# Dividing the first rows of an output projection unevenly over the DMA engines of a decode step

## The chip, the cores and the metric

The kernel runs on one core of a Trainium2 chip. The metric is the device time of one execution in microseconds (us). Before the change it is 197.57 us, the median of three runs that lie between 197.56 and 197.66. A profiled execution counts time from the first instruction to the last, and this span is 195.2 us.

Five engines of the core appear in the profile: PE (TensorE; its weight loads are listed apart as PEld), DVE (VectorE), ACT (ScalarE), POOL (GpSimd) and SP (SyncE). SP computes nothing here. It starts nearly all transfers between HBM and on-chip memory, one after the other, on one queue. The transfers themselves run on 16 DMA engines.

## What is computed

One decode step for four sequences: a layer norm, then attention over a window of the last 4096 cached positions (32 query heads, 8 key/value heads, head size 128) beside a SwiGLU feed-forward block, with both results added to the input.

```python
W = min(4096, max(256, Sk // 4))          # 4096
xn = layernorm(A_x)                       # [4, 1, 512]
q = (xn @ wq)                             # 32 heads of 128
k = k_cache[:, :, Sk - W:, :]             # 8 heads, each used by 4 query heads
v = v_cache[:, :, Sk - W:, :]
p = softmax(einsum("bhqd,bhkd->bhqk", q, k) * 128 ** -0.5)
o = einsum("bhqk,bhkd->bhqd", p, v)
attention = o.reshape(4, 1, 4096) @ wo    # wo is [4096, 512]
ffn = (silu(xn @ w_gate) * (xn @ w_up)) @ w_down
out = A_x + attention + ffn
```

Everything is in bf16 in HBM. The used windows of K and V are 32 MB each in the page's count (16 transfers of 2048 KB each), W_Q and W_O are 4 MB each, and the three feed-forward weights 1.75 MB each: 81.01 MB are read from HBM in one execution.

## The kernel before

The 32 pairs of sequence and key/value head are worked through in 16 duos. For each duo one transfer brings K and one brings V. PE transposes K tile by tile, DVE copies the transposes to on-chip memory, PE makes the scores, ACT takes the exponential, and PE multiplies with V. Each of K and V has two buffers, so the transfer for a duo can start when the duo before the last has left its buffer.

SP's list of transfers, cut to its last part:

```python
def load_v(j):
    if j > 0:
        eng.wait_ge(s_pv, j)               # the product with the V before last is done
    a = j % NSL * KVN
    eng.dma_start(VB[:, a:a + KVN], kv_ap(A_v_cache, j)).then_inc(d_v[j % NSL], 16)

def load_wo(n):                            # chunk n of W_O
    a, b = WO_CUTS[n], WO_CUTS[n + 1]      # WO_CUTS = (0, 16, 24, 28, 31, 32), in units of [128, 512]
    if b - a > REP:                        # REP = 4
        o, i = WO[:, a // REP:b // REP].rearrange("p k e n -> p k (e n)"), wo_ap[:, a // REP:b // REP]
    else:
        ...                                # a chunk within one key/value head
    eng.dma_start(o, i).then_inc(d_wo[n], 16)

# ... W_Q, the first K, W_gate and W_up are started before this ...
for j in range(1, NDUO):                   # NDUO = 16
    load_k(j)
    load_v(j - 1)
    if j == 1:
        eng.dma_start(WD[:], wd_ap).then_inc(d_wd, 16)
load_wo(0)                                 # units 0 to 15: half of W_O
load_v(NDUO - 1)                           # the last V
for n in range(1, len(d_wo)):
    load_wo(n)                             # units 16-23, 24-27, 28-30, 31
eng.wait_ge(s_y, 1)
eng.dma_start(out_ap[0], y[0:B, :]).then_inc(d_out, 16)
```

W_O lies in on-chip memory as `WO[128, 8, 4, 512]`: partition, key/value head, unit e within the head, output column. For one key/value head a partition's row is 2048 elements (4 KB) and lies in one piece in HBM.

PE's list from the end of the loop over duos on:

```python
eng.wait_ge(s_gu4, 1)
# ... four transposes for the feed-forward block, permute(0, ...) of heads 0 to 6 ...
# ... x and the 28 products with W_down go to ps_acc ...
eng.wait_ge(s_pc, 1)
for q in range(4):
    wo(q)                                  # heads 0 to 3; wo(0) waits for chunk 0 of W_O
pv(NDUO // 2, 0)                           # the last V: waits for its transfer, 1 + 64 products
wo(4)                                      # waits for chunk 1 (units 16-23)
wo(5)
eng.wait_ge(s_nrm, NDUO + 2)               # DVE has normalized the last product
permute(1, HKV - 1, HKV)
wo(6)                                      # waits for chunk 2 (units 24-27)
eng.wait_ge(s_pc, 2)                       # DVE has copied the last permutation
last = wo(7)                               # waits for chunks 3 (units 28-30) and 4 (unit 31)
last.then_inc(s_acc, 1)                    # DVE then makes y, and SP and ACT store it
```

`wo(q)` is four times two products of [128, 4] with [128, 256], and waits where a chunk begins. `norm` on DVE, which follows `pv`, is a reduction, a reciprocal and a product.

Of the kernel before, what the change touches and what calls it, by code (L numbers as in the profile page):

```python
# [10 lines left out]
def bass_parallel_sum__sliding_block_cached__swiglu_ffn__decode_kernel(  # L11
# [10 lines left out]
    out: bass.AP,  # L22
):
    B, _, D = A_x.shape
    _, HKV, Sk, Dh = A_k_cache.shape
    HQ = A_wq.shape[1] // Dh
    F = B_w_gate.shape[1]
# [23 lines left out]
    WO = sb("wo_sb", [128, HKV, REP, D], BF16)  # L51
# [53 lines left out]
    def sem(name):  # L105
        return nc.alloc_semaphore(name=name)
# [3 lines left out]
    d_wu = sem("d_wu")  # L110
    d_wd = sem("d_wd")
    d_out = sem("d_out")
    WO_CUTS = (0, 16, 24, 28, 31, 32)
    d_wo = [sem("d_wo%d" % q) for q in range(len(WO_CUTS) - 1)]
    s_xc = sem("s_xc")
    s_ss = sem("s_ss")
    d_k = [sem("d_k%d" % s) for s in range(NSL)]
# [33 lines left out]
    wo_ap = A_wo.rearrange("(k p e) n -> p k (e n)", k=HKV, e=REP)  # L151
# [3 lines left out]
    def kv_ap(cache, j):  # L155
        b, kv = 2 * j % B, 2 * j // B
        return cache[b:b + 2, kv, Sk - W:, :].rearrange("i (p t) d -> p i (t d)", t=NT)

    with nc.Block() as block:

        @block.gpsimd
        def _(eng):
            eng.memset(ident[:], 0.0)
            eng.memset(I4[:], 0.0)
            eng.memset(I4w[:], 0.0)
            eng.memset(XnT[:], 0.0)
            eng.memset(ones[:], 1.0)
            eng.drain()
            eng.affine_select(I4[:], I4[:], pattern=[[-1, B]], compare_op=ALU.not_equal,
                              fill=1.0, base=0, channel_multiplier=1)  # L170
            eng.affine_select(ident[:], ident[:], pattern=[[-1, 128]], compare_op=ALU.not_equal,
                              fill=1.0, base=0, channel_multiplier=1)
            eng.drain()
            eng.tensor_copy(I4w[:, 0:B], I4[:])
            for h in range(REP):
                eng.tensor_copy(sel[:, :, h, :], ident[:].rearrange("p (m e) -> p e m", e=REP))
            eng.memset(even[:], 0.0)
            eng.drain()
            eng.affine_select(even[:], even[:], pattern=[[-2, 64]], compare_op=ALU.not_equal,
                              fill=1.0, base=0, channel_multiplier=1)  # L180
            for w in (32, 16, 8, 4, 2, 1):
                eng.drain()
                eng.tensor_tensor(even[:, 0:w], even[:, 0:w], even[:, w:2 * w], ALU.add)
            eng.drain()
            eng.tensor_scalar(off[:, 0:1], even[:, 0:1], 30000.0, -30000.0, ALU.mult, ALU.add)
            eng.tensor_scalar(off[:, 1:2], even[:, 0:1], -30000.0, None, ALU.mult)
            eng.memset(P[:], 1.0)
            eng.memset(VB[:, (NSL - 1) * KVN:], 0.0).then_inc(s_const, 1)  # L188

        @block.sync  # L190
        def _(eng):
            def load_k(j):
                if j >= NSL:
                    eng.wait_ge(s_tr, NG * (j - NSL + 1))
                a = j % NSL * KVN
                eng.dma_start(KB[:, a:a + KVN], kv_ap(A_k_cache, j)).then_inc(d_k[j % NSL], 16)  # L196

            def load_v(j):
                if j > 0:
                    eng.wait_ge(s_pv, j)  # L200
                a = j % NSL * KVN
                eng.dma_start(VB[:, a:a + KVN], kv_ap(A_v_cache, j)).then_inc(d_v[j % NSL], 16)  # L202

            def load_wo(n):
                a, b = WO_CUTS[n], WO_CUTS[n + 1]
                if b - a > REP:
                    o, i = WO[:, a // REP:b // REP].rearrange("p k e n -> p k (e n)"), wo_ap[:, a // REP:b // REP]
                else:
                    e, k = a % REP, a // REP
                    o = WO[:, k, e:e + b - a].rearrange("p e n -> p (e n)")  # L210
                    i = wo_ap[:, k, D * e:D * (e + b - a)]
                eng.dma_start(o, i).then_inc(d_wo[n], 16)  # L212

            eng.dma_start(WQ[:, 0:2], wq_ap[:, 0:2]).then_inc(d_wq[0], 16)
            eng.dma_start(WQ[:, 2:4], wq_ap[:, 2:4]).then_inc(d_wq[1], 16)  # L215
            load_k(0)
            eng.dma_start(WG[:], wg_ap).then_inc(d_wg, 16)  # L217
            eng.dma_start(WU[:], wu_ap).then_inc(d_wu, 16)
            for j in range(1, NDUO):
                load_k(j)  # L220
                load_v(j - 1)
                if j == 1:
                    eng.dma_start(WD[:], wd_ap).then_inc(d_wd, 16)
            load_wo(0)
            load_v(NDUO - 1)
            for n in range(1, len(d_wo)):
                load_wo(n)
            eng.wait_ge(s_y, 1)
            eng.dma_start(out_ap[0], y[0:B, :]).then_inc(d_out, 16)
            eng.wait_ge(d_out, 32)  # L230
# [90 lines left out]
        def _(eng):  # L321
# [67 lines left out]
            def wo(q):  # L389
                for e in range(REP):  # L390
                    if REP * q + e in WO_CUTS:
                        eng.wait_ge(d_wo[WO_CUTS.index(REP * q + e)], 16)
                    for n in range(2):
                        last = mm(ps_acc[64 * n:64 * n + B, 0:256], OP[:, e, q, :],  # L394
                                  WO[:, q, e, 256 * n:256 * n + 256], start=False,
                                  stop=(q == HKV - 1 and e == REP - 1), skip_group_check=True)
                return last
# [17 lines left out]
            for t in range(NF):  # L415
                g, i = TG[t]
                for n in range(2):
                    mm(ps_acc[64 * n:64 * n + B, 0:256], guT[:, i, g, :], WD[:, t, 256 * n:256 * n + 256],
                       start=False, stop=False, skip_group_check=True)
            eng.wait_ge(s_pc, 1)  # L420
            for q in range(4):
                wo(q)
            pv(NDUO // 2, 0)
# [36 lines left out]
```

## Time and profile before

| what | value |
|---|---|
| time, median of three | 197.57 us |
| span of the profiled execution | 195.2 us |
| read from HBM | 81.01 MB, 415 GB/s over the span |
| share of 16 DMA engines' time on SP's queue | 97.5% |
| busy: PE, PEld, DVE, ACT | 80%, 73%, 60%, 10% |
| mean granted PE clock | 0.843 |

The profile's page gives the busy time of each engine, the same in 40 slices of time, the DMA queues, the chain of work that ended last, and the costliest groups of instructions with what ended the idle time before them. A queue's "packets" are the single pieces that a DMA engine moves; the trace keeps start, duration and size of each, and for each transfer's semaphore the time of each of the 16 steps by which it counts up.

### The profile page before, as it was taken

What the parts mean: (1) busy time and instruction counts of PE and PEld (TensorE: products, weight loads), DVE (VectorE), ACT (ScalarE), POOL (GpSimd) and SP (SyncE); (2) the same over time, 40 slices, a digit from 0 to 9 for tenths busy, and PEclk for the clock granted to TensorE, in tenths of its full rate; (3) what the DMA queues carried; (4) which work ended last, traced back from release to release, by engine and by line L of the source; (5) the groups of instructions that cost most, each with busy time, mean ns of one, the idle gap of its engine ahead of it and who ended that gap; (6) DMA issues with size and microseconds to landing.
All of it is one profiled execution on the core that took longest, in us unless ns stands there. A gap on an engine that the chain in (4) does not pass through costs nothing.

```text
span 195.2 us, 7471 instructions
## 1 busy us (share of the span) xinstructions
PE 155.5 (80%) x3335; PEld 142.6 (73%) x3335; DVE 117.2 (60%) x199; ACT 20.0 (10%) x42; POOL 11.6 (6%) x28
## 2 busy tenths in 40 slices
PE   0007569987999797987799779797989777999884
PEld 0012139977999797986799679797989777999662
DVE  3780099673848485756386638484857573858213
ACT  5201300101010101010101010101010101010100
POOL 6880000000000000000000000000000000000000
PEclk9999757996679788899579969797888995769699
DMA  6999999999999999999999999999999999999991
GB/s 216 430 430 450 423 420 426 434 436 433 430 433 433 433 433 430 433 430 433 433 430 430 430 430 430 430 430 430 433 430 433 430 430 430 430 430 411 448 397 60
DMA packets 6589, 81.10 MB, mean 415 GB/s; under 512 B 684, under 2 KB 824, under 8 KB 1848
## 3 DMA queue, kind: packets, MB, share of 16 engines
q1 hardware_dynamic: 6568, 81.01, 97.5%
q8 instruction: 5, 0.08, 0.1%
q10 hardware_dynamic: 16, 0.01, 0.0%
HBM read 81.01 MB, written 0.00 MB: 415 GB/s over the span
## 4 chain that ended last, share of the span: by engine, by line
DMA 65%; PE 31%; SPq 2%; issue 1%; DVE 0%
DMA kbuf<-in_A_k_cache_dram 43%; PE ps_kt L360 25%; DMA wu_sb<-in_B_w_up_dram 12%; DMA wo_sb<-in_A_wo_dram 10%; PE ps_o L379 2%; PE ps_s L367 2%; PE ps_den L348 1%; SPq L212 1%; PE ps_den L376 0%; PE ps_acc L394 0%; SPq L196 0%; SPq L217 0%; SPq L202 0%; DVE y_sb L318 0%; SPq L215 0%
## 5 line engine op out<-in xcount | busy, mean ns | idle before, releaser
L279 DVE COPY kT<-ps_kt 128x1024 bf16<-128x1024 bf16 x128 | 81.9, 686 | 34.9 <-PE ps_kt L360 34.6
L360 PE MATMUL ps_kt<-ident,kbuf 128*128 128x128 bf16 x1024 | 81.9, 259 | 12.0 <-DMA kbuf<-in_A_k_cache_dram 11.9
L360 PEld LDWEIGHTS ps_kt<-ident,kbuf 128*128 128x128 bf16 x1024 | 79.0, 120 | 14.2 <-issue 6.9
L379 PEld LDWEIGHTS ps_o<-p,vbuf 128*128 128x128 bf16 x1088 | 29.8, 96 | 3.1 <-issue 1.0
L379 PE MATMUL ps_o<-p,vbuf 128*128 128x8 bf16 x1088 | 29.9, 166 | 1.0 <-issue 1.0
L250 ACT ACTIVATE p<-ps_s,off 128x256 bf16<-128x256 f32 x32 | 13.4, 471 | 144.3 <-PE ps_s L367 144.3
L367 PE MATMUL ps_s<-qT,kT 128*128 x1024 | 28.0, 166 | 0.0
L367 PEld LDWEIGHTS ps_s<-qT,kT 128*128 128x128 bf16 x1024 | 26.9, 96 | 0.0
L285 DVE TENSOR_REDUCE den<-ps_den 128x8 f32<-128x512 f32 x17 | 11.8, 692 | 20.4 <-PE ps_o L379 20.4
L326 PE MATMUL ps_o<-i,tmp 4*128 4x4 f32 x4 | 0.6, 254 | 14.2 <-DVE tmp L269 14.2
L326 PEld LDWEIGHTS ps_o<-i,tmp 4*128 4x128 f32 x4 | 0.6, 206 | 14.2 <-POOL vbuf L188 14.2
L376 PE MATMUL ps_den<-p,ones 128*128 128x512 bf16 x17 | 6.5, 382 | 3.4 <-DMA vbuf<-in_A_v_cache_dram 3.4
L269 DVE TENSOR_SCALAR tmp<-tmp,st_rstd 4x512 f32<-4x512 f32 x1 | 7.9, 7864 | 0.1
L188 POOL MEMSET vbuf<- 128x8192 bf16 x1 | 6.9, 6921 | 0.0
L394 PE MATMUL ps_acc<-wo_sb,oP 128*4 128x256 bf16 x64 | 4.2, 272 | 1.0 <-DMA wo_sb<-in_A_wo_dram 0.9
L376 PEld LDWEIGHTS ps_den<-p,ones 128*128 128x128 bf16 x17 | 1.7, 97 | 4.3 <-issue 4.0
L289 DVE TENSOR_TENSOR oT<-ps_o,den 128x8 f32 (+1 forms) x17 | 2.8, 166 | 2.6 <-issue 2.5
L287 DVE RECIPROCAL den<-den 128x8 f32<-128x8 f32 x17 | 3.4, 203 | 1.2
L394 PEld LDWEIGHTS ps_acc<-wo_sb,oP 128*4 128x4 bf16 x64 | 2.6, 85 | 2.1 <-DVE oP L307 0.7
L336 PE MATMUL ps_kt<-wq_sb,xnT 128*32 128x512 bf16 x32 | 3.6, 627 | 0.3 <-DVE xnT L271 0.3
L348 PE MATMUL ps_den<-wu_sb,xnT 128*32 128x512 bf16 x16 | 1.9, 622 | 2.3 <-DMA wu_sb<-in_B_w_up_dram 2.3
L273 DVE COPY qT<-ps_kt 128x128 bf16<-128x128 bf16 x1 | 0.3, 291 | 5.5 <-PE ps_kt L341 5.5
(53 smaller groups left out, 33.3 us busy)
## 6 DMA issues: line engine op xcount, KB each, us to landing
kbuf<-in_A_k_cache_dram SPq DMA_DIRECT2D x16, 2048.0 KB, 14.0
vbuf<-in_A_v_cache_dram SPq DMA_DIRECT2D x16, 2048.0 KB, 17.1
wq_sb<-in_A_wq_dram SPq DMA_DIRECT2D x2, 2048.0 KB, 9.4
wo_sb<-in_A_wo_dram SPq DMA_DIRECT2D x1, 2048.0 KB, 21.7
wg_sb<-in_B_w_gate_dram SPq DMA_DIRECT2D x1, 1792.0 KB, 19.7
wu_sb<-in_B_w_up_dram SPq DMA_DIRECT2D x1, 1792.0 KB, 23.3
wd_sb<-in_B_w_down_dram SPq DMA_DIRECT2D x1, 1792.0 KB, 37.1
wo_sb<-in_A_wo_dram SPq DMA_DIRECT2D x1, 1024.0 KB, 18.2
```

Source lines behind the costliest of these rows:

```text
L188: eng.memset(VB[:, (NSL - 1) * KVN:], 0.0).then_inc(s_const, 1)
L250: last = eng.activation(P[:, :, h], S[:, :, h], ACT.Exp, scale=SCALE, bias=off[:, i:i + 1])
L269: eng.tensor_scalar(xn, xc, st_rstd[:, 0:1], None, ALU.mult).then_inc(s_xn, 1)
L279: eng.tensor_copy(KT[:, 1024 * g:1024 * g + 1024], kt_ps[g % 4].rearrange("p a b -> p (a b)")).then_inc(s_ev, 1)
L285: eng.tensor_reduce(den[:], ps_den[:].rearrange("p (t h) -> p h t", h=R2), AX.X, ALU.add)
L336: last = mm(q_ps[j][32 * g:32 * g + 32, :], XnT[:, c, :], w[:, g, 4 * j:4 * j + 4], start=(c == 0), stop=(c == NC - 1), skip_group_check=True)
L348: last = mm(o[32 * g:32 * g + 32, :], XnT[:, c, :], w[:, c].rearrange("p (m t) -> p m t", t=NF)[:, :, T4[g]:T4[g] + 4], start=(c == 0), st ...
L360: last = eng.transpose(kt_ps[g % 4][:, k, :], KB[:, a:a + 128], ident[:])
L367: last = mm(ps_S[:, R2 * t:R2 * (t + 1)], KT[:, 128 * t:128 * (t + 1)], q)
L376: mm(ps_den[:], ones[:], P[:].rearrange("p t h -> p (t h)"))
L379: last = mm(O_ps, VB[:, a:a + 128], P[:, t, :], start=(t == 0), stop=(t == NT - 1))
L394: last = mm(ps_acc[64 * n:64 * n + B, 0:256], OP[:, e, q, :], WO[:, q, e, 256 * n:256 * n + 256], start=False, stop=(q == HKV - 1 and e == ...
```

## The change

Chunk 0 of W_O was units 0 to 15 in one transfer of 128 partitions. Now units 0 to 3, head 0, are taken out of it and come ahead of the rest, in six transfers: the first half of each row (units 0 and 1, 2 KB) of partitions 0 to 79 in transfers of 25, 25, 25 and 5 partitions, the first half of the rows of partitions 80 to 127 in one transfer, and the second half of all 128 rows in one. All six count on one new semaphore, d_w0, and PE waits for all six (6 x 16 = 96) before the first product with W_O. The bytes are the same, and so is their place in the queue: before the last V.

A transfer of 128 partitions can be cut into 16 equal shares, one for each DMA engine. One of 25 or of 5 partitions cannot, but it can be cut into 5 equal shares. What the change is for is an uneven division of these rows over the DMA engines, so that engines that are behind get fewer bytes and others more.

```diff
-    WO_CUTS = (0, 16, 24, 28, 31, 32)
+    WO_CUTS = (4, 16, 24, 28, 31, 32)
     d_wo = [sem("d_wo%d" % q) for q in range(len(WO_CUTS) - 1)]
+    d_w0 = sem("d_w0")
...
                 load_v(j - 1)
                 if j == 1:
                     eng.dma_start(WD[:], wd_ap).then_inc(d_wd, 16)
+
+            o, i = WO[:, 0].rearrange("p e n -> p (e n)"), wo_ap[:, 0]
+            for a, b in ((0, 25), (25, 50), (50, 75), (75, 80)):
+                eng.dma_start(o[a:b, 0:2 * D], i[a:b, 0:2 * D]).then_inc(d_w0, 16)
+            eng.dma_start(o[80:128, 0:2 * D], i[80:128, 0:2 * D]).then_inc(d_w0, 16)
+            eng.dma_start(o[:, 2 * D:4 * D], i[:, 2 * D:4 * D]).then_inc(d_w0, 16)
             load_wo(0)
             load_v(NDUO - 1)
             for n in range(1, len(d_wo)):
...
             eng.wait_ge(s_pc, 1)
+            eng.wait_ge(d_w0, 96)
             for q in range(4):
                 wo(q)
             pv(NDUO // 2, 0)
```

## The prediction

> **What bounds the kernel now.** I read the page's slices of time first, then the DMA queues.
>
> ```profile
> PEclk9999757996679788899579969797888995769699
> DMA  6999999999999999999999999999999999999991
> GB/s 216 430 430 450 423 420 426 434 436 433 430 433 433 433 433 430 433 430 433 433 430 430 430 430 430 430 430 430 433 430 433 430 430 430 430 430 411 448 397 60
> ...
> q1 hardware_dynamic: 6568, 81.01, 97.5%
> q8 instruction: 5, 0.08, 0.1%
> q10 hardware_dynamic: 16, 0.01, 0.0%
> ```
>
> From the second slice to the last but one the DMA engines are 90% busy or more, at some 430 GB/s. The transfers bound the span, and the change moves the same bytes. So only two things can change: when the slowest DMA engine ends, and what waits for it. Next I read the end in narrow windows (the columns after the window are its length, busy time of PE, PEld, DVE, ACT and POOL with counts, granted clock, DMA share, GB/s).
>
> ```profile
> 189.00:190.50 1.50, 0.94 (x32) 0.79 (x30) 0.79 (x2) 0.00 (x0) 0.00 (x0) 1.00 1.00 402
> 190.50:191.00 0.50, 0.50 (x14) 0.33 (x8) 0.27 (x2) 0.00 (x0) 0.00 (x0) 1.00 0.70 250
> 191.00:191.50 0.50, 0.49 (x11) 0.26 (x8) 0.08 (x1) 0.00 (x0) 0.00 (x0) 1.00 0.26 104
> 191.50:192.00 0.50, 0.49 (x8) 0.18 (x4) 0.46 (x4) 0.00 (x0) 0.00 (x0) 1.00 0.24 92
> 192.00:192.50 0.50, 0.12 (x4) 0.12 (x6) 0.14 (x1) 0.00 (x0) 0.00 (x0) 1.00 0.10 35
> ```
>
> All 16 are busy until 190.5; then the share is 0.26 and 0.24, about four of sixteen. Four engines end late. The steps of the transfers' semaphores say the same: the last chunk of W_O counts twelve steps from 190.96 to 191.17 and four from 192.37 to 192.59; the last V counts twelve from 185.92 to 186.15 and four from 187.36 to 187.58.
>
> Why four? The trace's records of single packets have no engine's number, but a 16 KB packet takes 611 ns and the next of its engine starts 3 or 4 ns before it ends, so sixteen chains can be followed by their phases. Five packets of 16 KB belong to the instruction queue (q8 above). They start at 31.76, 39.85, 45.96, 184.44 and 190.60, each falls into another chain, and the chain then runs late for good. For the fourth: the fetch takes 0.86 us and the data packet after it 1.16 instead of 0.61, a loss of 1.41 us. The fifth falls into an engine whose data is through.
>
> Last, PE's timeline at the end, for what waits for the late engines:
>
> ```profile
> 185.76 1.91 PE L394 MATMUL ps_acc<-wo_sb,oP 128*4 128x256 bf16 x32
> 187.62 0.10 PEld L376 LDWEIGHTS ps_den<-p,ones 128*128 128x128 bf16 x1 [0.24 <-DMA vbuf<-in_A_v_cache_dram]
> 187.63 1.87 PEld L379 LDWEIGHTS ps_o<-p,vbuf 128*128 128x128 bf16 x64
> 189.63 0.69 DVE L285 TENSOR_REDUCE den<-ps_den 128x8 f32<-128x512 f32 x1 [6.56 <-PE ps_o L379]
> 190.15 1.04 PE L394 MATMUL ps_acc<-wo_sb,oP 128*4 128x256 bf16 x16 [0.56 <-DMA wo_sb<-in_A_wo_dram]
> 190.68 0.17 DVE L289 TENSOR_TENSOR oT<-ps_o,den 128x8 bf16<-128x8 f32 x1
> 191.12 0.26 PE L385 MATMUL ps_kt<-oT,sel 128*128 128x16 bf16 x4
> 192.35 0.36 PEld L394 LDWEIGHTS ps_acc<-wo_sb,oP 128*4 128x4 bf16 x8 [0.66 <-DVE oP L307]
> 192.38 0.60 PE L394 MATMUL ps_acc<-wo_sb,oP 128*4 128x256 bf16 x8 [0.39 <-DMA wo_sb<-in_A_wo_dram]
> ```
>
> The last V, complete at 187.58, releases PE at 187.62. PE could have gone on at about 187.4: it waits 0.24 us and no more. Then two paths run nearly level: V to product to norm to permutation to DVE's copy, which releases PE at 192.35, and W_O's chunk 3, complete at 192.25, at 192.38. An earlier W_O alone buys nothing; the last V must be earlier too.
>
> [...] the 4-partition load of x and a 4-partition store, all 16 packets of q10, are four data packets and four semaphore packets each. No packet shows which engines. [...]
>
> **The change part by part.** Packets of 4, 3 and 1 KB follow each other on an engine every 155, 118 and 42 ns in this trace, so 1 KB is 38 ns and a 2 KB packet is estimated at 42 + 38 = 80 ns. A semaphore packet takes 6 ns of its engine.
>
> Removed: head 0's share of chunk 0, eight 4 KB rows per engine, 8 x 155 = 1.24 us on every engine.
>
> Added on all engines: 48 half rows in 16 shares, 3 each; 128 half rows, 8 each: 11 x 80 ns = 0.88 us, and two more semaphore packets, 0.01 us. Engines 5 to 15 thus gain 1.24 - 0.89 = 0.35 us.
>
> Added on engines 0 to 4 alone: 80 half rows in five shares, 16 x 80 ns = 1.28 us, and four semaphore packets, 0.02 us. They lose 0.35 - 1.30, that is 0.95 us.
>
> SP: six issues in place of none, at the 0.4 to 0.6 us that its issues take here, some 3 us from 161.0 on. The next, the last V, waits until 171.36 anyway. The later chunks may be issued some us later (the last one's issue already takes 2.95 us[...]), but they are issued 10 us or more ahead of their turn. PE's extra wait is for data that lands near 177, 8 us early. Both free.
>
> So all turns on whether the four late engines are among 0 to 4.
>
> (a) None is. The last V is complete at 187.58 - 0.35 = 187.23 on the late engines and 186.15 + 0.95 = 187.10 on engines 0 to 4. PE is free at about 187.4, so it gains 0.2 and not 0.35. The path through norm and copy moves by the same 0.2 (192.35 to 192.13); chunk 3 is there at 191.90 and chunk 4 at 192.24, before the product that needs it. 197.57 - 0.2 = 197.35.
>
> (b) At least one is. If it is only the engine that got the fetch at 184.44, its V lands at 187.36 + 0.95 = 188.31 instead of the 187.58 of the latest: +0.73. Chunk 1 follows at 189.89 + 0.95 = 190.84 against 190.11, again +0.73; chunk 3 at 192.98 against a copy path of 192.35 + 0.73 = 193.08. The end moves by 0.73: 198.30. If one of the three old late engines is among them, up to 0.95: 198.52.
>
> Which? At the very start each engine begins its first W_Q packet at a time of its own: 1.769, 1.782, 1.809, 1.813, 1.848, 1.874 and so on, to 2.729. Following the chains with gaps of only 2 to 5 ns and the known order of packet sizes, I get the fetches at these places of that starting order, counted from 0: the first at 5 or 3 (a tie of two chains), the second at 15, the third at 11, the fourth at 2, the fifth at 1. If engines start in the order of their numbers, the three that are late from the first third on are 5 (or 3), 11 and 15. That fits a design with engines 0 to 4 as the ones with time to spare. But the fourth, which falls behind only at 184.44, just as the last V is moving, would be engine 2, within the five that get more. That the start follows the numbers is my choice; no record proves it. Any other order leaves a random chance of (11x10x9x8)/(16x15x14x13) = 0.18 that none of four is in five.
>
> **The rivals.** First, the design is right and all late engines are above 4: case (a). For it speaks the size: 0.95 + 0.35 = 1.30 us between the groups almost fills the 1.4 us lag, so with this division both groups would end within 0.15 us of each other. Against it speaks the fourth chain. I give it about 0.33. Second, the fourth late engine is among 0 to 4: (b), 0.60. Third, [...] small packets are absorbed, and nothing moves: 197.5 to 197.7, for about 0.07. A fourth, that the six issues or the extra wait hold the end up, would cost up to 1 us; the slack of 6 and 8 us speaks against it. A shifted clock window (PE runs at half clock from 182.65 to 185.64) could add a few tenths either way.
>
> **Range and chances.** The weights are 0.60 at 198.3, 0.33 at 197.35, the rest between. Predicted: 198.2 us; 197.2 to 198.6 should hold it 8 times in 10. Two per cent are 3.95 us, far beyond every case: faster 0.01, within 0.98, slower 0.01.
>
> **What would show it.** The steps of the last V's semaphore: in (b) one step stands alone near 188.3, and PE's products with the last V begin there, with more idle time before them; in (a) all sixteen lie between 185.6 and 187.3. The DMA share after 190.5: in (b) it falls slowly, with one engine alive to about 193.3; in (a) it stays high to about 191.5 and all ends near 192.2. In both, three old late chains should be 0.35 us earlier. Head 0's half rows must show as 2048 B packets, 27 on each of five engines and 11 on each of the others. The prediction is wrong if the shares are not so, if the fourth fetch falls on another engine, or if PE's work before 187.4 shifts.

## The result, and the profile after

The changed kernel takes 198.59 us (median of six runs, 197.85 to 199.15) against 197.61 for before in the same comparison: a ratio of 1.0051, 95% interval 1.0029 to 1.0073. It is slower, by about 1 us. The prediction said 198.2, with 197.2 to 198.6 as range: the result lies at the range's upper edge, and the predicted loss of 0.6 us was too small. A second comparison, of 22 runs, gave 198.32 us against 197.74, and 1.0029 (1.0009 to 1.0048); the two intervals overlap, and both say slower.

The profiled run is the fastest of the six (197.85 us, span 195.7 us instead of 195.2), so its trace shows about 0.5 us of the loss. The page's slices of time and queues:

```profile
DMA  6999999999999999999999999999999999999992
GB/s 229 429 429 435 422 432 439 415 449 429 422 429 429 439 435 429 429 429 429 429 429 429 435 429 429 429 432 432 435 442 432 429 429 429 439 407 357 445 403 84
...
q1 hardware_dynamic: 6748, 81.01, 97.7%
q8 instruction: 5, 0.08, 0.2%
```

The bytes are the same. The division is the intended one, as far as the trace tells. A load of 128 partitions has 16 steps at its semaphore. The 4-partition load of x, for which DVE waits until 16, has four from 2.08 us on, one for each of its four semaphore packets, and one at 1.37, before its first data packet at 1.70; so this first one must count for all the rest. The semaphore of the six transfers has 56 steps, 4 x 6 + 2 x 16, for a wait until 96; four of them come at 161.50 to 162.55, each within 0.2 us of the end of an issue of 25 or 5 partitions. So I read five engines for each of these transfers. Which five, no packet shows: that they are 0 to 4, as the prediction and the expectations have it, was the author's assumption. What has changed is the fourth and fifth slice from the end: 407 and 357 GB/s (the second of them is 176.1 to 181.0 us), where there were 430 and 411. The DMA engines are as busy there as elsewhere. The end in the same windows as before:

```profile
189.00:190.50 1.50, 1.42 (x57) 1.32 (x53) 0.04 (x1) 0.00 (x0) 0.00 (x0) 1.00 0.99 406
190.50:191.00 0.50, 0.49 (x10) 0.41 (x12) 0.50 (x1) 0.00 (x0) 0.00 (x0) 1.00 0.97 383
191.00:191.50 0.50, 0.50 (x11) 0.21 (x6) 0.35 (x3) 0.00 (x0) 0.00 (x0) 1.00 0.88 330
191.50:192.00 0.50, 0.33 (x8) 0.26 (x8) 0.16 (x1) 0.00 (x0) 0.00 (x0) 1.00 0.53 209
192.00:192.50 0.50, 0.50 (x8) 0.17 (x4) 0.46 (x3) 0.00 (x0) 0.00 (x0) 1.00 0.34 119
```

This is the picture that the prediction drew for its case (a): the share stays high to 191.5, then more than four engines work on (0.53, 0.34 where there was 0.24, 0.10), and all are through by 192.5. The uneven division does what it was for. But nothing ends earlier: the last chunk of W_O counts seven steps from 191.26 to 191.65 and nine from 192.40 to 192.97, where there were twelve until 191.17 and four until 192.59. Now PE's timeline, first one line of before and then after:

```profile
177.89 0.39 PE L376 MATMUL ps_den<-p,ones 128*128 128x512 bf16 x1
```

```profile
178.62 0.39 PE L383 MATMUL ps_den<-p,ones 128*128 128x512 bf16 x1 [0.39 <-DMA vbuf<-in_A_v_cache_dram]
186.43 2.08 PE L401 MATMUL ps_acc<-wo_sb,oP 128*4 128x256 bf16 x32
188.44 0.10 PEld L383 LDWEIGHTS ps_den<-p,ones 128*128 128x128 bf16 x1 [0.22 <-issue]
190.46 0.69 DVE L292 TENSOR_REDUCE den<-ps_den 128x8 f32<-128x512 f32 x1 [6.65 <-PE ps_o L386]
190.51 1.04 PE L401 MATMUL ps_acc<-wo_sb,oP 128*4 128x256 bf16 x16
191.72 0.26 PE L392 MATMUL ps_kt<-oT,sel 128*128 128x16 bf16 x4 [0.17 <-DVE oT L296]
192.80 0.60 PE L401 MATMUL ps_acc<-wo_sb,oP 128*4 128x256 bf16 x8 [0.29 <-DVE oP L314]
```

Two things are new. The product with the last V but one (first line after) waits for its transfer and starts at 178.62; it was 177.89. PE carries this delay on, and the product with the last V starts at 188.44 instead of 187.62, now with only "issue" ahead of it: in this run PE is what is late. The chain that ended last agrees. Before, it came to the end through a chunk of W_O; now it goes through the last V but one and then PE:

```profile
160.27 18.23 DMA vbuf<-in_A_v_cache_dram
178.50 0.12 issue
178.62 0.39 PE ps_den L383
```

The last V itself, complete at 188.02 by its semaphore's steps instead of 187.58, comes 0.4 us before that. The last V but one is complete at 178.50 (177.77 before), although its place in the queue is ahead of everything that was changed.

The records of single packets show where the time goes. Mean duration in ns of the packets that start in each half microsecond:

```
            176.0   176.5   177.0   177.5   178.0   178.5
before 4 KB   159     159     159     159     159     159
after  2 KB    84      90     142     133     128      85
after  4 KB     -     215     291     266     232     159
```

From 176.7 to 178.5 us packets of every size take up to 1.8 times as long on average, even the last three 16 KB packets of the last V but one on the late engines (887 ns on average instead of 611). In windows of 1 us (the last two columns are DMA share and GB/s), first the kernel before, then after:

```profile
177.00:178.00 1.00, 1.00 (x18) 0.86 (x16) 1.00 (x3) 0.00 (x0) 0.00 (x0) 1.00 0.97 397
178.00:179.00 1.00, 1.00 (x37) 0.89 (x36) 1.00 (x3) 0.00 (x0) 0.00 (x0) 1.00 1.03 426
```

```profile
177.00:178.00 1.00, 1.00 (x22) 1.00 (x19) 1.00 (x2) 0.00 (x0) 0.00 (x0) 1.00 0.98 229
178.00:179.00 1.00, 0.61 (x13) 0.33 (x10) 1.00 (x3) 0.00 (x0) 0.00 (x0) 1.00 1.02 344
```

A full DMA share at 229 GB/s: the engines are not idle, each packet is slow. I call this the slow stretch. It does not begin with the half rows of head 0. The first of them starts at 175.68, and 134 of them start and take their 84 ns before the first slow one among them, at 176.71; from 0.2 us later on and until 178.4 every packet that starts is slow, on whatever engine. In the other kernels with a slow stretch it is the same: it begins 0.5 to 0.9 us after the first of the new packets and then takes in all packets within 0.2 us. What delays the start of the stretch no record shows.

### The profile page after: what moved, and what is told of

Read it like the earlier page. It is cut to its first block, busy times and chain, and to the rows that moved or that the text cites. A ratio compares the mean times of both kernels' runs of the same rounds, so it can differ in the third digit from the quotient of the medians.

```text
span 195.7 us, 7477 instructions
## 1 busy us (share of the span) xinstructions
PE 154.8 (79%) x3335; PEld 141.0 (72%) x3335; DVE 116.7 (60%) x199; ACT 20.0 (10%) x42; POOL 11.6 (6%) x28
## 4 chain that ended last, share of the span: by engine, by line
DMA 56%; PE 37%; issue 3%; DVE 1%; SPq 1%; ACT 0%; DVEq 0%
DMA kbuf<-in_A_k_cache_dram 35%; PE ps_kt L367 24%; DMA wu_sb<-in_B_w_up_dram 12%; DMA vbuf<-in_A_v_cache_dram 9%; PE ps_o L386 5%; PE ps_s L374 4%; PE ps_acc L425 2%; PE ps_acc L401 1%; PE ps_den L355 1%; PE ps_den L383 1%; ACT p L257 0%; DVE oP L314 0%; DVE den L292 0%; SPq L197 0%; SPq L218 0%
## 5 line engine op out<-in xcount | busy, mean ns | idle before, releaser
L367 PE MATMUL ps_kt<-ident,kbuf 128*128 128x128 bf16 x1024 | 80.1, 254 | 10.9 <-DMA kbuf<-in_A_k_cache_dram 10.8
L367 PEld LDWEIGHTS ps_kt<-ident,kbuf 128*128 128x128 bf16 x1024 | 76.7, 117 | 13.7 <-issue 8.3
```

Source lines behind the costliest of these rows:

```text
L367: last = eng.transpose(kt_ps[g % 4][:, k, :], KB[:, a:a + 128], ident[:])
```

## The experiments

Each was compared with runs of before made beside it, whose median was 197.61 (first comparison), 197.74, 197.76 or 197.79 us; the ratio is to those runs and is not the quotient of the medians. "V(14)" is the last V but one, "V(15)" the last, each with the time at which its semaphore has all 16 steps in the profiled run. "Packets" is the mean duration at the worst of the half microseconds, for packets that take 159 ns (4 KB), 121 ns (3 KB) or 84 ns (2 KB) undisturbed. The expectations speak of an engine's own share of the partitions, and of others' shares (theory A). That was the author's assumption: no record has a packet's engine or address. What the runs compare is how the transfers are cut.

| kernel | median us (runs) | ratio, 95% interval | V(14) | V(15) | packets |
|---|---|---|---|---|---|
| before | 197.61 to 197.79 | | 177.77 | 187.58 | 159 |
| changed, first comparison | 198.59 (6) | 1.0051, 1.0029 to 1.0073 | 178.50 | 188.02 | 142, 291 |
| changed, again | 198.32 (22) | 1.0029, 1.0009 to 1.0048 | 178.75 | 188.30 | 150, 297 |
| even, half rows, 80 and 48 | 198.48 (22) | 1.0041, 1.0026 to 1.0056 | 178.38 | 188.48 | 136, 219 |
| uneven, whole rows | 199.55 (6) | 1.0097, 1.0065 to 1.0129 | 179.32 | 189.31 | 299 |
| even, whole rows, 128 | 197.74 (14) | 1.0017, 0.9992 to 1.0042 | 177.86 | 188.09 | 159 |
| half rows, 128 | 198.01 (22) | 1.0016, 0.9997 to 1.0035 | 177.80 | 187.93 | 84 |
| even, whole rows, 80 and 48 | 199.74 (7) | 1.0085, 1.0054 to 1.0116 | 179.26 | 189.56 | 326 |
| extra on five engines, rows four apart | 197.67 (22) | 0.9987, 0.9973 to 1.0001 | 177.74 | 187.78 | 121 |
| the same extra, neighbouring rows | 198.27 (14) | 1.0031, 1.0009 to 1.0054 | 178.46 | 188.20 | 163, 214 |
| even, eight of 16 | 200.00 (6) | 1.0101, 1.0075 to 1.0127 | 179.75 | 189.97 | 365 |
| even, whole rows, 128, other pitch | 197.91 (22) | 1.0005, 0.9986 to 1.0025 | 177.78 | 187.76 | 159 |
| pieces after the rest | 198.30 (22) | 1.0026, 1.0015 to 1.0036 | 178.02 | 188.40 | 143, 291 |

### The changed kernel again

No edit.

> The changed kernel itself, once more. Theory 1 (the engine that gets an instruction fetch is not the same in every execution, and the uneven division makes its identity count): times spread over about 1 us again, between 197.8 and 199.2, while before stays within 0.3 us; in its profile, the engines that move 27 half rows may or may not be among the late ones. Theory 2 (a fixed cost of the new transfers alone): the times lie within 0.3 us of each other, near 198.5. Both expect the slow stretch of 2 KB and 4 KB packets near 176.5 to 178.5 us again, and the last V but one complete near 178.5 instead of 177.8.

The slow stretch was there again. Theory 1, that chance decides which engines get the fetches and the uneven division makes that count, lost its sign: before, on the same chip, also spread from 197.33 to 199.66, though only two of its 51 runs were above 199.2, and the evenly divided kernel of the next experiment spread from 198.10 to 200.26. Theory 2 fell too, since the times do not lie within 0.3 us. Of the changed kernel's 22 runs eight lie between 199.20 and 199.54 and fourteen between 197.99 and 198.44. The profiled run is one of the eight. Its windows at the end (granted clock third from the right):

```profile
186.00:188.00 2.00, 2.00 (x22) 1.25 (x20) 0.00 (x0) 0.00 (x0) 0.00 (x0) 0.50 0.91 367
188.00:190.00 2.00, 2.00 (x24) 1.14 (x20) 0.00 (x0) 0.00 (x0) 0.00 (x0) 0.61 1.03 422
```

and of its timeline:

```profile
186.77 3.27 PE L401 MATMUL ps_acc<-wo_sb,oP 128*4 128x256 bf16 x32
189.97 0.10 PEld L383 LDWEIGHTS ps_den<-p,ones 128*128 128x128 bf16 x1 [0.22 <-issue]
```

The 32 products with W_O run at half clock and take 3.27 us; they took 2.08 in the profile after and 1.91 before. The last V is complete at 188.30, but PE comes to it at 189.97. So in this run the upper group is a matter of PE's clock, in work that the late V(14) has put on the path that sets the end. That all eight are of this kind was not traced, and a late V(14) is not needed for such times: in the three kernels below that have head 0 in a load of its own and no slow stretch, 4 of 14, 3 of 22 and 4 of 22 runs are above 199 us too. In before it is 6 of 145 over the three later comparisons.

### Even halves

```diff
-            for a, b in ((0, 25), (25, 50), (50, 75), (75, 80)):
+            for a, b in ((0, 80), (80, 128)):
                 eng.dma_start(o[a:b, 0:2 * D], i[a:b, 0:2 * D]).then_inc(d_w0, 16)
-            eng.dma_start(o[80:128, 0:2 * D], i[80:128, 0:2 * D]).then_inc(d_w0, 16)
```

> Head 0 still in half rows of 2 KB, but every transfer divided evenly over 16 engines (80, 48 and 128 partitions). If half rows make the slow stretch (2 KB read out of every 4 KB): it is here too, packets of 2 KB take 120 to 150 ns, the last V but one is complete near 178.5, and the time is 198.0 to 198.4 with a small spread. If the five-engine transfers make it: 2 KB packets take 84 ns throughout, the last V but one is complete near 177.8, and the time is 197.6 to 197.7, the same as before. Theory 1 expects a spread of at most 0.3 us.

The slow stretch stayed (2 KB packets of 136 ns), V(14) came at 178.38, and the time is 198.48. So neither few engines nor an uneven division is needed for it. That read like a verdict for half rows, and was none: transfers of 80 and 48 partitions are also new here, and the next runs separate the two. PE waits 0.61 us for the last V in this trace: here that transfer is late, and not PE.

### Uneven division in whole rows

```diff
-            for a, b in ((0, 25), (25, 50), (50, 75), (75, 80)):
-                ...
+            for a, b in ((0, 25), (25, 40), (40, 120), (120, 128)):
+                eng.dma_start(o[a:b], i[a:b]).then_inc(d_w0, 16)
```

> The uneven division kept (14 rows of head 0 on each of engines 0 to 4, 5 or 6 on each other), but in whole rows of 4 KB: transfers of 25, 15, 80 and 8 partitions. If half rows make the slow stretch: none here, 4 KB packets take 159 ns, the last V but one is complete near 177.8, and the times are 197.4 where no late engine is among engines 0 to 4 and 198.3 to 198.5 where one is, median near 198. If the five-engine transfers make it: 4 KB packets of 250 ns or more for about 2 us, and times as those of the changed kernel, median near 198.6. Theory 1 expects a spread near 1 us either way.

The stretch is longer and the time worse, 199.55: half rows are not the cause. One thing in my design was wrong: I had taken the 15 partitions to go to five engines. The semaphore counts 47 steps, 6 + 16 + 16 + 9. Read as in the trace after, 16 for 15 partitions is 15 engines and the step at the issue, and 9 for 8 partitions is eight and that step. So the five loaded engines carried 10 to 12 rows and not 14: five of 25, five of 80, and at most one each of 15 and 8.

### Even division in whole rows

```diff
-            for a, b in ((0, 25), (25, 50), (50, 75), (75, 80)):
-                ...
+            eng.dma_start(o, i).then_inc(d_w0, 16)
```

> Head 0 in a transfer of its own, whole rows, 128 partitions, ahead of the other three heads: neither half rows nor an uneven division. Every theory expects the time of before within 0.1 us (197.6) and a spread of at most 0.3 us. Should it be slower, the cost lies in the cut of chunk 0 or in the new semaphore.

No packet is slow, and the ratio's interval contains 1. The cut of chunk 0 and the new semaphore cost nothing that these runs resolve. The spread, 197.53 to 199.59, is far above the 0.3 us that I expected, by the four runs above 199 us.

### Half rows in transfers of 128

```diff
-            for a, b in ((0, 25), (25, 50), (50, 75), (75, 80)):
-                ...
+            for a in (0, 2 * D):
+                eng.dma_start(o[:, a:a + 2 * D], i[:, a:a + 2 * D]).then_inc(d_w0, 16)
```

> Head 0 in half rows of 2 KB, first halves then second halves, both transfers of all 128 partitions[...]. Theory A (the slow stretch comes from engines that write partitions of another engine's share): no slow stretch, 2 KB packets take 84 ns throughout, the last V but one is complete near 177.8, time within 0.1 us of before. Theory B (it comes from reading 2 KB out of 4 KB rows): packets of 120 ns and more from 176 to 178 us, the last V but one near 178.3, time 0.6 us above before.

2 KB packets of 84 ns throughout, V(14) at 177.80. The median is 0.25 us above before, more than the 0.1 us that I allowed, with an interval that contains 1. Half rows do not make the stretch: theory B falls.

### Whole rows in transfers of 80 and 48

```diff
-            for a, b in ((0, 25), (25, 50), (50, 75), (75, 80)):
-                ...
+            for a, b in ((0, 80), (80, 128)):
+                eng.dma_start(o[a:b], i[a:b]).then_inc(d_w0, 16)
```

> Head 0 in whole rows, divided evenly over 16 engines, but in transfers of 80 and 48 partitions[...]. Theory A: a slow stretch, 4 KB packets of 200 ns and more for 1 us or longer, the last V but one near 178.3, time 0.5 to 1 us above before. Theory B: none, 159 ns, time as before. A third theory, that only an uneven division makes it, also expects none here.

The bytes and the packet size of the transfer of 128, and no division uneven by the steps: 80 partitions have 16 in the uneven division in whole rows, 48 have 16 in the profile after. What differs is the cut. Which engine then moves which rows, writes which partitions and reads which addresses, no record shows. Windows of this kernel:

```profile
176.00:177.00 1.00, 1.00 (x16) 1.00 (x14) 0.84 (x2) 0.00 (x0) 0.00 (x0) 0.73 1.30 356
177.00:178.00 1.00, 1.00 (x22) 1.00 (x19) 1.00 (x3) 0.00 (x0) 0.00 (x0) 1.00 0.92 188
178.00:179.00 1.00, 0.34 (x7) 0.17 (x3) 1.00 (x3) 0.00 (x0) 0.00 (x0) 1.00 0.94 254
179.00:180.00 1.00, 0.40 (x16) 0.51 (x18) 0.57 (x1) 0.00 (x0) 0.00 (x0) 1.00 1.05 266
```

188 GB/s at a DMA share of 0.92, and PE idle from 178 on because V(14) is complete only at 179.26. This is the changed kernel's loss, larger (199.74), without anything uneven. The first slow packet starts at 176.37. No engine is through with its share of the transfer of 80 by then, five rows if 16 engines share them evenly (the first started at 175.72, and five rows take 5 x 155 ns), so that transfer alone is enough to begin the stretch. In this traced run the 32 products with W_O took 3.34 us instead of 1.91, much as in the second trace of the changed kernel (3.27, at a granted clock of 0.50 to 0.61), which is part of its 200.09 us.

### An extra load for five engines, in rows four apart

The kernel before, with bytes that nobody uses:

```diff
+            for a in (0, 1, 2, 3, 32, 33, 34, 35):
+                eng.dma_start(WQ[a:a + 17:4, 0, 0:1536], wo_ap[a:a + 17:4, 0, 0:1536]).then_inc(d_w0, 16)
             load_wo(0)
```

> The kernel before with an addition that computes nothing: ahead of chunk 0, eight transfers of 5 partitions with a stride of 4 (3 KB rows, into a part of the W_Q buffer that is no longer read). They load engines 0 to 4 alone, 8 packets of 118 ns each, 1.0 us more[...]. If no engine that gets an instruction fetch is among 0 to 4: the extra is hidden in the lag of the others, no slow stretch, time within 0.15 us of before. If one is (case b of the prediction): the last V has one step near 188.4 and the time is 0.7 to 1.0 us above before. If few-partition transfers slow all engines by themselves: packets of 160 ns and more for 3 KB.

```profile
176.00:177.00 1.00, 0.81 (x14) 0.57 (x11) 1.00 (x3) 0.00 (x0) 0.00 (x0) 1.00 1.02 413
177.00:178.00 1.00, 0.00 (x0) 0.11 (x2) 1.00 (x3) 0.00 (x0) 0.00 (x0) 1.00 1.00 410
```

No slow stretch beside forty such packets (121 ns each), and the ratio is 0.9987, 0.9973 to 1.0001: a full microsecond more for five engines costs nothing that these runs resolve. The last chunk of W_O counts seven steps from 191.07 to 191.38, five from 192.06 to 192.22 and four from 192.41 to 192.69: the five engines with the extra, and apart from them the four late ones. By case (b) of the prediction it would have cost 0.7 to 1.0 us; that is excluded here. In the traces of the changed kernel (second comparison), of the uneven whole rows and of the last experiment below the same seven, five and four stand apart.

### The same extra in neighbouring rows

```diff
-            for a in (0, 1, 2, 3, 32, 33, 34, 35):
-                ...
+            for a, b in ((0, 25), (25, 40)):
+                eng.dma_start(WQ[a:b, 0, 0:1536], wo_ap[a:b, 0, 0:1536]).then_inc(d_w0, 16)
```

> The same as the addition of own rows, the same engines, 8 packets of 3 KB for each of engines 0 to 4, but as transfers of 25 and 15 neighbouring partitions[...]. Theory A: a slow stretch (3 KB packets over 150 ns, 4 KB and 16 KB packets stretched beside them), the last V but one later than 178.0, time 0.3 to 1 us above the kernel with own rows. Theory B: no difference between the two.

3 KB packets of 163 ns (but only two start in that half microsecond, and 17 in the one before took 146), 4 KB packets of 214, V(14) at 178.46, and 1.0031 in place of 0.9987. (Here too the 15 partitions went to 15 engines: 22 steps, 6 + 16. The five loaded engines carried 5 or 6 packets and not 8, and the others one each at most. So the same 40 rows lay lighter on the five, and cost more.) What differs is the cut, rows four apart or neighbouring ones; a write side and a read side are not told apart by this pair.

### Eight transfers of 16 partitions

```diff
-            for a, b in ((0, 25), (25, 50), (50, 75), (75, 80)):
-                ...
+            for a in range(0, 128, 16):
+                eng.dma_start(o[a:a + 16], i[a:a + 16]).then_inc(d_w0, 16)
```

> Head 0 in whole rows, in eight transfers of 16 neighbouring partitions, one row for each engine: an even division[...]. Theory A (write side, engines that share a target hold each other up): the strongest dose, 4 KB packets of 300 ns and more beside each other, the last V but one later than 178.3, time 0.8 to 2 us above before. A theory of the uneven division, or of few-partition transfers, expects the time of before within 0.2 us.

```profile
177.00:178.00 1.00, 1.00 (x22) 1.00 (x19) 1.00 (x3) 0.00 (x0) 0.00 (x0) 1.00 1.09 205
178.00:179.00 1.00, 0.40 (x8) 0.22 (x4) 1.00 (x2) 0.00 (x0) 0.00 (x0) 1.00 0.93 188
179.00:180.00 1.00, 0.00 (x0) 0.11 (x2) 0.73 (x2) 0.00 (x0) 0.00 (x0) 1.00 1.01 303
180.00:181.00 1.00, 0.91 (x36) 0.90 (x36) 0.00 (x0) 0.00 (x0) 0.00 (x0) 1.00 1.06 270
```

The stretch lasts five microseconds and a 4 KB packet takes up to 365 ns on average. Eight equal transfers and yet the highest median of all, 200.00 us (its interval overlaps those of 199.74 and 199.55): this speaks against every theory that needs an uneven division. It agrees with theory A and does not show a shared target: the first 37 of these packets still take 159 ns, and all are slow only after 176.34.

### One transfer of 128, another pitch in HBM

Head 0 gets wrong rows here; the amount of work is the same.

```diff
-            for a, b in ((0, 25), (25, 50), (50, 75), (75, 80)):
-                ...
+            wide = A_wo.rearrange("r n -> (r n)")[0:128 * 2560].rearrange("(p c) -> p c", p=128)
+            eng.dma_start(o, wide[:, 0:4 * D]).then_inc(d_w0, 16)
```

> Head 0 in one transfer of 128 partitions[...], but read from HBM at a pitch of 5 KB instead of 4 KB[...] (the weights of head 0 are then the wrong rows; the work is the same). Theory A, write side: no slow stretch, 4 KB packets of 159 ns, time within 0.15 us of before. A read-side theory (the addresses in HBM that are read together make the stretch): packets of 200 ns and more for about 2 us and a time 0.5 us or more above before.

159 ns throughout, ratio 1.0005. A pitch of 5 KB in HBM instead of 4 does not make the stretch in a transfer of 128. That the read side is no cause at all is not shown: which addresses are read together is in no record, and no other pitch was tried. A shared target on the write side is in no record either and was the author's guess.

### The pieces behind the rest of chunk 0

```diff
+            load_wo(0)
             o, i = WO[:, 0].rearrange("p e n -> p (e n)"), wo_ap[:, 0]
             ...
-            load_wo(0)
             load_v(NDUO - 1)
```

> The changed kernel with its six transfers behind the rest of chunk 0 instead of ahead of it. If the slow stretch belongs to the six transfers, it moves to about 179 to 182 us, away from the end of the last V but one, which is then complete near 177.8 and releases PE about 0.7 us sooner; the last V is still late, 188.0 to 188.3, because the stretch costs every engine the same as before. Expected: PE waits for the last V by 0.4 us or more again, the time is 0.1 to 0.4 us below the changed kernel and 0.3 us or more above before. If instead the loss came only through the late start of PE, the time is that of before.

```profile
178.69 1.75 PE L386 MATMUL ps_o<-p,vbuf 128*128 128x8 bf16 x64
186.03 2.37 PE L401 MATMUL ps_acc<-wo_sb,oP 128*4 128x256 bf16 x32
188.45 0.10 PEld L383 LDWEIGHTS ps_den<-p,ones 128*128 128x128 bf16 x1 [0.34 <-DMA vbuf<-in_A_v_cache_dram]
193.13 0.60 PE L401 MATMUL ps_acc<-wo_sb,oP 128*4 128x256 bf16 x8 [0.41 <-DMA wo_sb<-in_A_wo_dram]
```

The stretch moved with its transfers, to 180 to 182.7 us, and V(14) came at 178.02. PE now waits 0.34 us for the last V, complete at 188.40. But the product with it starts at 188.45, as in the profile after (188.44), and the time did not fall: 198.30 against 198.32. The gain that I expected is not there. A late last V is enough to hold this point up. It does so in the traced runs of four other kernels with a stretch: even half rows (PE waits 0.61 us for it), uneven whole rows (0.38), the extra in neighbouring rows (1.37) and eight of 16 (1.20). A late PE held it up in both runs of the changed kernel and in even whole rows of 80 and 48.

## Why the prediction was wrong

**What bounds the kernel.** Right. The end follows the slowest transfers, and the point where PE takes up the last V decides: 187.62 before, 188.44 in the profile after.

**Which engines are late.** Wrong, and the choice on which the weights stood. I took the five loaded engines to be 0 to 4, and from the order in which engines began their first packet the fourth fetch to be on engine 2. In every trace of an uneven division in which the groups can be told apart, the four late engines are not among the five loaded ones (seven, five and four steps at the end), and a microsecond more on the five costs nothing that could be resolved (0.9987). So the starting order is not the order of the numbers, or the loaded five are not 0 to 4, or the fetch did not lie on the chain that I followed; which, stays open. Case (b), to which I gave 0.60, did not happen; that its 198.3 came near the measured time is chance.

**The term that was mis-sized.** With case (a) the sum was: the eleven engines without more rows gain 0.35 us, the last V is complete at 187.23. It came at 188.02. The step that failed is "a 2 KB packet is estimated at 42 + 38 = 80 ns", taken for the whole of the six transfers. Undisturbed it was right: a packet's record is 84 ns long, and the next starts after 80. But that held only for the first microsecond and wherever a transfer of 128 was cut in two. In the slow stretch the packet took up to 142 ns on average, and packets that I had not touched slowed with it: 4 KB from 159 to 291, the last 16 KB of V(14) from 611 to 887. The predicted 0.35 us of gain became 0.44 us of loss at the last V (188.02 - 187.58): 0.79 us in all, for the profiled run. (The last V is complete between 187.58 and 188.09 in the kernels without the stretch, so some tenths of this are the lag's own scatter; V(14), at 177.74 to 177.86 without and 178.38 or later with it, unless the pieces come behind, is the cleaner mark.)

**What the few-partition transfers cost besides.** I counted packets per engine and did not ask what the cut by partitions costs. The runs show it. Five kernels have no slow stretch: before, head 0 in whole rows of 128, in half rows of 128 and at another pitch, and the extra in rows four apart (4, 3 and 2 KB packets of 159, 121 and 84 ns). Seven that load 5 to 80 neighbouring partitions at a time all have one (4 KB packets of 214 to 365 ns on average at the worst), and 16 neighbouring rows at a time give the longest packets (365 ns). That engines which write in each other's shares hold each other up was the author's theory; the runs agree with it and do not show it. Why all packets of the core slow together, and 0.5 to 1.0 us after the first new packet, is open as well.

**What was ahead in the queue.** I held everything issued before the six transfers for safe. V(14)'s late engines still had 16 KB packets to move when the stretch began, and V(14) came 0.73 us later. In the profile after that made PE late by itself, which no part of the sum had.

**SP's issues and PE's extra wait.** Right: the last V is issued at 170.12 after a free wait, the six issues took 0.27 to 0.54 us each, and head 0 lands at 179.3, 7 us before its use.

**Half clock.** I allowed a few tenths for it. Two traced runs, of the changed kernel (granted clock 0.50 to 0.61) and of even whole rows of 80 and 48, lost 1.36 and 1.43 us in 32 products (3.27 and 3.34 instead of 1.91 us), and PE had no slack left there.

No kernel beats before by more than its uncertainty. The five engines do have a microsecond to spare (0.9987 with the extra), but in both divisions that were tried, half rows (1.0051 and 1.0029) and whole rows (1.0097), handing them more of W_O's rows cost more than it returned.

## What to carry to other kernels

When a transfer is cut by partitions, ask not only how many engines it uses but what the cut itself does to the packets: one of 128 rows into 80 and 48 cost 0.85% here, a cut of the same rows along the free axis nothing that could be resolved. A DMA share near 1.0 at half the GB/s was the sign of it here, and single packets' durations name the stretch. To test whether some engines have slack, load them with bytes that nobody uses, in a cut that leaves the packets as short as before (121 ns for 3 KB in rows four apart here, 163 in neighbouring ones), before you move real work to them.

## What was not expected of the hardware

- The slowing takes in every engine: in the slow stretch all packets that start are slow, even 16 KB packets of the transfer of 128 that was ahead in the queue (887 ns on average instead of 611), and over 1 us the core as a whole fell to 229 GB/s in the changed kernel, and to 188 in even whole rows of 80 and 48 and in eight of 16, from some 430. It begins 0.5 to 1.0 us after the transfers that bring it.
- One 16 KB packet of the profile's instruction queue (0.88 to 0.97 us long in before) costs the DMA engine that moves it 1.41 to 1.42 us, for good, in the four of the five fetches of before that are followed by data. The four engines that lag at its end are these four; in the uneven kernels whose traces tell the groups apart, none of the four late ones is among the five loaded ones. Which rule picks the engine stays open.
- 32 products took 3.27 us instead of 1.91 at a granted clock of 0.50 to 0.61, and 3.34 in another traced run: more than a microsecond, once PE has no slack ahead of the last V. Whether it makes the runs above 199 us, which kernels without a slow stretch have too, and what sets its start, was not tried.
